# One load queue, some exponentials over four banks, and a new task list in a transformer layer with segment memory

## The chip, the cores and the metric

The kernel runs on one core of a Trainium2 chip. The core has five engines that each work through an instruction queue of their own: TensorE (PE, matrix products), VectorE (DVE), ScalarE (ACT, functions such as exp and tanh), GpSimd (POOL) and SyncE (SP, which here only issues DMA transfers). They are held together by semaphores. Matrix products read SBUF, the on-chip memory, and write PSUM, eight banks of 512 fp32 numbers on each of 128 partitions. ACT can issue DMA transfers too, and while it does so it computes nothing.

The metric is the device time of one execution in microseconds (us). Three runs of the kernel before gave 301.33, 301.71 and 301.79 us; the median is 301.71.

## The reference

One sequence of 2048 tokens, 640 wide, in bf16. A layer with two residual steps:

```python
h  = x + attention(layernorm(x))          # 32 heads of 20, output projection wo
h2 = h + silu(layernorm(h) @ w1) @ w2     # w1: 640 x 1728, w2: 1728 x 640
```

The attention treats the sequence as four segments of 512 tokens, one after the other. In each segment and head

```python
a_dot = softmax(causal(q @ k.T / sqrt(20))) @ v
a_mem = (phi(q) @ M) / (phi(q) @ z + 1e-6)       # phi(t) = t + 1 if t > 0 else exp(t)
o     = sigmoid(beta) * a_mem + (1 - sigmoid(beta)) * a_dot
M    += phi(k).T @ v ;  z += sum(phi(k))
```

so a segment needs the memory `M`, `z` of the segments before it, and nothing else from them.

## The kernel before

**Blocks and segments.** Tokens are held in 16 blocks of 128; segment s holds blocks 4s to 4s+3. The normalised tokens are transposed so that the 640 features lie on partitions (`hT`, `xT`: five chunks of 128). Blocks 0 to 3 are transposed on PE against an identity tile (`n1_tp`, L783) and evicted from PSUM (`n1_te`, L792); all later ones by DMA transposes that SP issues (`n1_tr`, `n2_tr`, L798).

**Heads.** 32 heads of 20 do not fit 32-row strips evenly, so the query and key weights are rearranged on arrival (`re_wq0` to `re_wk4`, `rearr` L678, the copies at L697 and L699): the 20 columns of 20 heads go to five chunks of four strips each, and the columns of the other 12 heads fill the remaining 12 rows of each strip. After a projection (`pr`, L861; segment 0 in two halves of 256 tokens, `x` and `y`) and its eviction (`qe`, L869 on ACT, L870 on DVE), small DMA copies gather these 12 "virtual" heads into their own tile (`vt`, `virt` L900, the transfer at L901; tile `w_sb` in segment 0, `QKV` after it). So there are eight head groups of four heads; groups 0 to 4 read the projections directly, groups 5 to 7 wait for the copies.

**A visit.** For a head group and some key blocks, `scores` (L921) writes the scores of four heads into four PSUM banks side by side (`qk`, L938), ACT takes their exponential into SBUF (`e`, L949), POOL zeroes the part above the diagonal (`mk`, L960). The exponential of a visit is two instructions, one for banks 0 and 1 and one for banks 2 and 3, of 2 x 512 or 2 x 384 numbers. `av` (L981) multiplies with the values, `oe` evicts and scales (L994 on ACT, L996 on DVE), `tn` (L1010, L1014) adds the memory part and turns tokens back onto partitions, `nm` divides (L1027 to L1047), `ad` (L1055, POOL) adds both parts. Segment 0 is visited in halves (`0x` to `7x`, then `0ya`, `0yb` to `7yb`); segments 1 to 3 as `8a, 8b, 8e` and so on, with `8 + g` for group g of segment 1. There are 84 visits.

**Memory.** `pha`, `phb` and `ex` form phi of queries and keys; `kt` transposes phi(k) by DMA, `mz` (L1103) multiplies it with the values, `ma` adds to the fp32 memory, `mb` (POOL, L1139) masks it with constants (`mt`, `mm`, `mzc`) that POOL builds once.

**Back.** `ot` transposes the attention output by DMA (L1156), `wo` projects it (L1164), `rs` adds the residual, `n2_` normalises, `h1` (L1199, its narrow tail L1193) and `th`, `s` (L1208, L1214) form the silu, `h2` (L1241) and `o` (L1254) finish, `out` stores (L1259). `v` (L826) and `ve` (L836, L837) are the value projection and its eviction.

**The order.** Nothing is scheduled by the machine. `ORDER` is one written list of some 1,480 task names; `schedule` (L287) takes them in this order, and each engine gets its tasks in the order in which the list names them. A name may carry an engine (`/A` ACT, `/D` DVE, `/G` POOL, `/S` SP) and, after a colon, the slots (PSUM banks or buffers) that its results take. Names of different engines that stand side by side need not run at the same time. `Tracker.add` puts in the semaphore waits that the data and the slots demand. `fill36` and the like are matmuls of zeros (L618) that keep PE at work.

**The loads before.** SP issues x0, the query weights, the first 384 rows of the key weights, the first 384 rows of the value weights, x4 to x7, `wo`, `beta` and later loads. ACT issues x1, x2 and x3, the other 256 rows of the key weights and the other 256 of the value weights, ahead of its first computation.

Of the kernel before, what the change touches and what calls it, by code (L numbers as in the profile page):

```python
# [1316 lines left out]
```

## Time and profile before

| | |
|---|---|
| median of three runs | 301.71 us |
| span of the profiled execution, first to last instruction | 300.4 us |
| PE busy | 288.8 us, 96% |
| ACT busy | 223.1 us, 74% |
| DVE busy | 222.4 us, 74% |
| POOL busy | 142.7 us, 48% |
| read from and written to HBM | 10.41 MB, 2.62 MB |
| share of the chain that ended last | PE 77%, DVE 12%, DMA 4%, ACT 3% |

The profile is of one execution. Its device time as the runs count it is not given apart; the median of the runs stands 1.3 us above its span, which covers what lies ahead of the first instruction and behind the last. The rows of a stretch give its length and then the busy time of PE, of PE's weight loads, of DVE, ACT and POOL, the granted clock, the busy share of the DMA engines and GB/s. In a list in order of time a row has start, length, engine, line, operation, tiles, shapes and how many instructions were merged; in brackets stands how long the engine was idle before and what ended that. PE's rows overlap, since a matmul's end is modelled with its way through the array; a row of several matmuls, divided by their number, tells what one costs in a stream. "SPq" and "ACTq" are the two queues' DMA issues.

### The profile page before, as it was taken

The page shows a single profiled execution, that of the slowest core. Times are in us where ns is not written, and L with a number is a line of the kernel's source. Part 1 is how long each engine was busy: PE and PEld are TensorE (multiplying, and loading weights), DVE is VectorE, ACT ScalarE, POOL GpSimd, SP SyncE. Part 2 cuts the span into 40 slices and gives each one's busy share as a digit, 9 for nine tenths or more (in the row PEclk, how much of TensorE's full clock was granted, in tenths as well). Part 3 has the DMA queues.
Part 4 walks back from the last instruction along what each step waited for, and adds up shares of the span by engine and source line. Part 5 has one row for each costly group of instructions (what it writes and reads, how often), then busy time and mean ns, then how long its engine had stood idle before and what let it go on. Part 6 is the DMA issues. An engine that isn't in the chain of part 4 may idle for free.

```text
span 300.4 us, 7527 instructions
## 1 busy us (share of the span) xinstructions
PE 288.8 (96%) x2999; PEld 171.4 (57%) x3023; DVE 222.4 (74%) x515; ACT 223.1 (74%) x318; POOL 142.7 (48%) x272
## 2 busy tenths in 40 slices
PE   7799899999999999999999999999999999999996
PEld 5576455455665555556654454566565557764574
DVE  6899988878569689989588866857947787735622
ACT  1898999999998999999589999978777840015400
POOL 6689743534635646855455455564673531200000
PEclk9999999999999999999999999999999999999999
DMA  7994544325454301251742300243120023230002
GB/s 256 362 350 77 116 117 126 89 56 135 85 88 102 63 2 19 42 95 23 94 138 44 79 9 20 39 85 78 47 65 24 2 44 68 46 86 23 0 9 81
DMA packets 49250, 24.66 MB, mean 82 GB/s; under 512 B 39168, under 2 KB 47616, under 8 KB 49216
## 3 DMA queue, kind: packets, MB, share of 16 engines
q1 hardware_dynamic: 46060, 20.52, 31.0%
q10 hardware_dynamic: 3156, 3.67, 4.0%
q8 instruction: 24, 0.39, 0.5%
q14 instruction: 10, 0.08, 0.1%
HBM read 10.41 MB, written 2.62 MB: 43 GB/s over the span
## 4 chain that ended last, share of the span: by engine, by line
PE 77%; DVE 12%; DMA 4%; ACT 3%; issue 2%; SPq 0%; POOL 0%; DVEq 0%; ACTq 0%
PE ps_all L1241 21%; PE ps_all L1199 16%; PE ps_all L861 9%; PE ps_all L1164 8%; PE ps_all L938 7%; PE ps_all L981 6%; PE ps_all L826 5%; DMA sT<-in_A_wk_dram 3%; PE ps_all L1010 2%; ACT PT L949 2%; PE ps_all L1014 2%; PE ps_all L1103 2%; DVE stt L747 2%; DMA oT<-otok 1%; DVE on L1047 1%
## 5 line engine op out<-in xcount | busy, mean ns | idle before, releaser
L949 ACT ACTIVATE PT<-ps_all 128x1024 bf16<-128x1024 f32 (+1 forms) x168 | 157.0, 992 | 15.2 <-PE ps_all L938 13.6
L960 POOL TENSOR_SCALAR_AFFINE_SELECT PT<-PT 128x512 bf16<-128x512 bf16 x128 | 82.7, 649 | 66.9 <-ACT PT L949 63.4
L1241 PE MATMUL ps_all<-w_sb,sT 128*128 128x320 bf16 (+2 forms) x462 | 65.1, 295 | 0.0
L1199 PE MATMUL ps_all<-hT,w_sb 128*128 128x512 bf16 (+1 forms) x314 | 61.6, 335 | 1.5 <-DVE sT L1214 0.4
L1208 ACT ACTIVATE th<-ps_all 128x512 f32<-128x512 f32 (+2 forms) x70 | 34.9, 517 | 36.1 <-PE ps_all L1199 27.4
L1241 PEld LDWEIGHTS ps_all<-w_sb,sT 128*128 128x128 bf16 x462 | 43.3, 98 | 18.9 <-issue 2.1
L1214 DVE SCALAR_TENSOR_TENSOR sT<-th,ps_all 128x512 bf16<-128x512 f32 (+2 forms) x70 | 37.8, 558 | 14.9 <-ACT th L1208 14.2
L1199 PEld LDWEIGHTS ps_all<-hT,w_sb 128*128 128x128 bf16 x325 | 29.6, 98 | 24.9 <-issue 2.8
L1254 DVE SCALAR_TENSOR_TENSOR x_tok<-ps_all,x_tok 128x640 bf16<-128x640 f32 (+3 forms) x18 | 13.3, 748 | 22.4 <-PE ps_all L1241 22.3
L747 DVE BATCH_NORM_STATS2 stt<-x_tok 128x6 f32<-128x320 bf16 x62 | 27.1, 479 | 2.3 <-DMA x_tok<-in_A_x_dram 2.0
L768 POOL TENSOR_TENSOR rst<-rst,eps_c 128x1 f32<-128x1 f32 x32 | 18.3, 573 | 15.4 <-DVE rst L762 13.6
L1164 PE MATMUL ps_all<-wo_sb,oT 128*128 128x320 bf16 x160 | 24.1, 300 | 0.2
L1055 POOL TENSOR_TENSOR otok<-on 128x320 bf16<-128x320 bf16 x24 | 19.0, 799 | 11.0 <-DVE on L1047 11.0
L981 PE MATMUL ps_all<-PT,Vx 128*32 128x256 bf16 (+3 forms) x576 | 23.5, 287 | 0.7 <-DVE Vx L837 0.3
L1047 DVE TENSOR_TENSOR on<-ps_all,rd 128x640 bf16<-128x640 f32 x24 | 19.8, 824 | 0.8
L1164 PEld LDWEIGHTS ps_all<-wo_sb,oT 128*128 128x128 bf16 x160 | 14.8, 98 | 7.8 <-issue 2.0
L870 DVE CAST QK<-ps_all 128x512 bf16<-128x512 f32 x23 | 15.7, 685 | 4.7 <-PE ps_all L861 4.3
L996 DVE TENSOR_SCALAR oTs<-ps_all,lsc 128x512 bf16<-128x512 f32 (+1 forms) x28 | 17.0, 618 | 2.2 <-PE ps_all L981 2.1
L826 PE MATMUL ps_all<-wv_sb,xT 128*128 128x320 bf16 x120 | 18.3, 299 | 0.3 <-ACT Vx L836 0.3
L981 PEld LDWEIGHTS ps_all<-PT,Vx 128*32 128x32 bf16 x576 | 12.2, 96 | 11.1 <-issue 5.1
L774 DVE TENSOR_SCALAR xn_rot<-x_tok,mvt,rst 128x640 bf16<-128x640 bf16 x32 | 15.2, 477 | 4.1 <-POOL rst L768 3.5
L861 PE MATMUL ps_all<-xT,wqr 128*128 128x512 bf16 x69 | 17.2, 379 | 0.7 <-DVE otok L1029 0.2
(88 smaller groups left out, 351.0 us busy)
## 6 DMA issues: line engine op xcount, KB each, us to landing
w_sb<-in_B_w_dram SPq DMA_DIRECT2D x5, 432.0 KB, 9.3
w_sb<-in_B_w_dram SPq DMA_DIRECT2D x3, 480.0 KB, 3.8
out_dram<-x_tok SPq DMA_DIRECT2D x9, 160.0 KB, 1.9
x_tok<-in_A_x_dram SPq DMA_DIRECT2D x2, 640.0 KB, 11.5
out_dram<-x_tok ACTq DMA_DIRECT2D x6, 160.0 KB, 1.8
QKV<-QK SPq DMA_DIRECT2D x12, 72.0 KB
sT<-in_A_wq_dram SPq DMA_DIRECT2D x1, 800.0 KB, 7.6
wo_sb<-in_A_wo_dram SPq DMA_DIRECT2D x1, 800.0 KB, 13.8
```

The lines of the kernel that those rows point to most:

```text
L747: T.add(DV, lambda e, hh=hh: e.bn_stats(out=stt[:, s, 6 * hh:6 * hh + 6], in_=xb[:, 320 * hh:320 * hh + 320]), reads=R((xa, xsub)), writes ...
L826: fns.append(lambda e, c=c, hh=hh: e.matmul(bank(ps, hh)[:, 0:320], lhsT=xT_[:, c, 128 * i:128 * i + 128], rhs=wv_sb[:, c, 320 * hh:320 * ...
L861: fns = [lambda e, kc=kc: e.matmul(bank(ps)[:, lo:hi], lhsT=wt[:, kc, c, :], rhs=xT_[:, kc, lo:hi], start=(kc == 0), stop=(kc == NC - 1)) ...
L949: T.add(AC, lambda e: e.activation(out=pt[:, pta.slot, q0:q0 + 2, 0:width], in_=sc3[:, b0:b0 + 2, 0:width], func=ACT.Exp, scale=SCALE), re ...
L960: T.add(PO, lambda e: e.affine_select(out=v, in_=v, pattern=[[0, 4], [1, 128]], compare_op=ALU.is_ge, fill=0.0, base=0, channel_multiplier ...
L981: fns.append(lambda e, j=j, r=r, h=h, pa=pa, pt=pt, co=co, q0=q0, ji=ji: e.matmul(bank(po)[32 * r:32 * r + 32, q0:hi], lhsT=Vx[:, vx.slot, ...
L1047: T.add(DV, lambda e: e.tensor_tensor(out=on[:, ona.slot, :, :].rearrange("p b (x e) -> p b x e", e=DH), in0=v[:, :, :, 0:DH], in1=r2.unsq ...
L1164: fns.append(lambda e, c=c, hh=hh: e.matmul(bank(ps, hh)[:, 0:320], lhsT=oT[:, c, 128 * i:128 * i + 128], rhs=wo_sb[:, c, 320 * hh:320 * h ...
L1199: fns = [lambda e, c=c: e.matmul(bank(ps)[:, lo:hi], lhsT=w1_sb[:, c, 128 * f:128 * f + 128], rhs=hT[:, c, lo:hi], start=(c == 0), stop=(c ...
L1208: T.add(AC, lambda e: e.activation(out=th[:, tha.slot, lo:hi], in_=bank(ps)[:, lo:hi], func=ACT.Tanh, scale=0.5), reads=R((ps, [0])), writ ...
L1214: T.add(DV, lambda e: e.scalar_tensor_tensor(out=sT[:, f, lo:hi], in0=th[:, tha.slot, lo:hi], scalar=1.0, in1=bank(ps)[:, lo:hi], op0=ALU. ...
L1241: fns.append(lambda e, f=f, t0=t0, fr=fr, hh=hh, n=n: e.matmul(bank(pa, hh)[:, 0:n], lhsT=sT[:, f, t0:t0 + 128], rhs=w2_sb[:, fr, c0 + 320 ...
```

## The change

1. All loads of the head are issued by SP, in the order x0, x1, query weights, key weights (one transfer in place of two), x2 and x3, value weights (still two), then x4 to x7, `wo`, `beta`. ACT issues none of them. In segment 0 the value projection waits for the first part of the value weights ahead of its first six matmuls and for the second part ahead of the other four, instead of for both at once.
2. A name such as `e2x+` in the list stands for one exponential over all four banks of the visit; the pairs `e2x0`, `e2x2` are then gone. 45 of the 84 visits are written so.
3. `ORDER` is another list. PE's tasks keep their order in the main, with the head and the last output blocks arranged differently; `fill12` is gone, `fill2` stands at the end, with a `fill5`. On DVE, ACT, POOL and SP many tasks have other places, 59 tasks have another engine (eight `qe` from ACT to DVE and seven the other way, nine `oe`, seven `vt` from SP to ACT and two the other way, the loads of x12 and of the first part of `w2` from ACT to SP, others), and banks and slots differ.

```diff
 ORDER = """
-halfc:0 epsc iota mt2 x1:3 vpad1 zpad sel w2z/G:0 x0:7 w_q:0 epsg0 mt0 mta0 x2:5,0 w_k1 w_k0 w_wv1:0 warm n1_st3/A:0,0
-n1_st0/D:1 n1_st1/D:6 mtb0 mm0 n1_r0/G n1_r1/D n1_ap0:0 n1_ap1:1 n1_st2/D:2 mm2 n1_r2/D re_wq0/D:0 re_wq2/D n1_r3/G
...
+zpad:0 iota fill36:1 warm x0:7 x1:0 w_q:0 w_k x2:4,1 w_wv0:0 epsc n1_st1/D:3,0 halfc n1_r1/D w_wv1 n1_st0/A:5 n1_r0/D
+sel x4:2,10,3,5 w_wo:0 n1_ap1:1 n1_tp1:2 n1_te1/A:0 beta n1_ap0:0 mt2 n1_tp0:0 n1_te0/A re_wq4/D:0 pr040x:1 qe040x/A:0
+re_wq1/D re_wq0/D pr010x:0 re_wk2/A:0 re_wq3/D re_wq2/D pr000x:4 qe010x/A:0 qe000x/A:0 re_wk1/D pr011x:5 qe011x/A
+re_wk0/D pr001x:6 qe001x/A mt3 re_wk3/D n1_st2/D:1 n1_r2/G mt1 qk1x0:0 e1x2:4 pr021x:7 qe021x/A:0 e1x0 n1_st3/D:5
+n1_ap2:3 mt0 pr030x:6 qk0x0:2 pr020x:7 qe030x/A:0 e0x2:0 n1_r3/D re_wk4/D n1_tp2:0 qe020x/D n1_ap3:2 n1_te2/D pr041x:6
...
+mk10b_384 kt10:0 n1_ap8:0 phb100 ex121:0 h2_1_1 mk11a_0 vt11/S n1_tr8 qk11b0:2 phb120 n1_ap11:3 n1_tr9 n1_tr11 e11b+:6
+mk10e_256 mk11b_0 pha121:2 rs3 n2_st3:7 tn8:0 nm8:0,0 ex141:1 h2_1_2 h2_1_3 o1 mb04:0 mzc2 mb01:0 qk12a0:2 wo2:0
+e12a+:0 ex140:2 av10:6 rs2 oe10/D:0 qk12b0:2 e12b2:5 mz13:7 ma13 phb121 vt14/S vt12/S pr220:0 e12b0 vt16/S qk13a0:4
...
 """.split()
+
+
+ONE_EXP = {row.partition("+")[0] for row in ORDER if row[0] == "e" and "+" in row}
...
     load_x(0, 1, -100, 2.30, "fix", (SP,))
-    load_x(1, 1, -100, 2.33, "fix", (AC,))
-    load_x(2, 2, -97, 4.79, "fix", (AC,))
-    load_w("q", wraw[:, 0, :, :], cw(A_wq), -99, 6.58, [(sT0, ["q"])], "fix", (SP,))
-    load_w("k0", wraw[:, 1, 0:3, :], cw(A_wk[0:384, :]), -99, 4.0, [(sT0, ["k0"])], "fix", (SP,))
-    load_w("k1", wraw[:, 1, 3:5, :], cw(A_wk[384:640, :]), -99, 2.7, [(sT0, ["k1"])], "fix", (AC,))
-    load_w("wv0", wv_sb[:, 0:3, :], cw(A_wv[0:384, :]), -95, 4.96, [(W["wv"], [0])], "fix", (SP,))
-    load_w("wv1", wv_sb[:, 3:5, :], cw(A_wv[384:640, :]), -95, 4.96, [(W["wv"], [1])], "fix", (AC,))
+    load_x(1, 1, -100, 2.33, "fix", (SP,))
+    load_w("q", wraw[:, 0, :, :], cw(A_wq), -96, 6.58, [(sT0, ["q"])], "fix", (SP,))
+    load_w("k", wraw[:, 1, :, :], cw(A_wk), -95, 6.58, [(sT0, ["k"])], "fix", (SP,))
+    load_x(2, 2, -97, 4.79, "fix", (SP,))
+    load_w("wv0", wv_sb[:, 0:3, :], cw(A_wv[0:384, :]), -99, 4.0, [(W["wv"], [0])], "fix", (SP,))
+    load_w("wv1", wv_sb[:, 3:5, :], cw(A_wv[384:640, :]), -99, 2.7, [(W["wv"], [1])], "fix", (SP,))
...
-            rr, ww = [(sT0, ["k0", "k1"] if wi else ["q"])], [(W[k], [c])]
+            rr, ww = [(sT0, ["k"] if wi else ["q"])], [(W[k], [c])]
...
-                T.run(PE, fns, R((xTa, [i]), (W["wv"], [0, 1])), R((ps, [0])))
+                if s == 0:
+                    T.run(PE, fns[:6], R((xTa, [i]), (W["wv"], [0])), R((ps, [0])))
+                    T.run(PE, fns[6:], R((xTa, [i]), (W["wv"], [1])), R((ps, [0])))
+                else:
+                    T.run(PE, fns, R((xTa, [i]), (W["wv"], [0, 1])), R((ps, [0])))
...
-                for q0 in range(r0, r0 + nr, 2):
+                nq = 4 if f"e{name}" in ONE_EXP else 2
+                for q0 in range(r0, r0 + nr, nq):
                     def e_ex(eng, q0=q0, r0=r0, sca=sca):
                         b0 = sca.slot + q0 - r0
-                        T.add(AC, lambda e: e.activation(out=pt[:, pta.slot, q0:q0 + 2, 0:width],
-                                                         in_=sc3[:, b0:b0 + 2, 0:width], func=ACT.Exp, scale=SCALE),
-                              reads=[("ps", b0 + q) for q in range(2)], writes=R((pta, [q0])))
...
+                        T.add(AC, lambda e: e.activation(out=pt[:, pta.slot, q0:q0 + nq, 0:width],
+                                                         in_=sc3[:, b0:b0 + nq, 0:width], func=ACT.Exp, scale=SCALE),
+                              reads=[("ps", b0 + q) for q in range(nq)], writes=R((pta, range(q0, q0 + nq, 2))))
```

The list numbers used below: `n1_st`, `n1_r`, `n1_ap` are a block's statistics (L747, L750 on DVE; L739, L742 on ACT), its reciprocal root (L762 or L765, then the power at L768 on POOL) and the normalisation (L774); `sel` is the identity tile (L633); `w2z` the memset at L601.

198 lines of the change are left out of this document (95 added, 103 removed).

## The prediction

> **What bounds the kernel now.** I read the page's first part, then stretches cut by hand, then the chain of waits, then the first microseconds in order of time.
>
> ```profile
> span 300.4 us, 7527 instructions
> PE 288.8 (96%) x2999; PEld 171.4 (57%) x3023; DVE 222.4 (74%) x515; ACT 223.1 (74%) x318; POOL 142.7 (48%) x272
> ```
> ```profile
> 10.93:29.40 18.47, 17.91 (x184) 13.06 (x184) 18.11 (x61) 17.11 (x35) 16.75 (x52) 1.00 0.93 249
> 29.40:40.00 10.60, 9.05 (x153) 4.84 (x152) 9.86 (x30) 9.94 (x15) 8.41 (x14) 1.00 0.56 126
> 40.00:80.00 40.00, 38.83 (x480) 22.19 (x486) 31.46 (x85) 39.01 (x58) 16.72 (x29) 1.00 0.43 98
> 80.00:130.00 50.00, 48.95 (x568) 28.19 (x571) 40.36 (x88) 47.00 (x65) 29.25 (x46) 1.00 0.31 58
> 130.00:200.00 70.00, 68.91 (x687) 37.49 (x693) 54.35 (x117) 61.81 (x83) 37.56 (x64) 1.00 0.32 58
> 200.00:297.90 97.90, 97.12 (x872) 59.66 (x876) 60.11 (x114) 43.76 (x59) 27.48 (x48) 1.00 0.19 45
> 297.90:300.40 2.50, 0.04 (x1) 0.00 (x0) 0.37 (x2) 0.00 (x0) 0.00 (x0) 1.00 0.35 111
> ```
> The columns are the stretch, its length, then busy time of PE, weight load, VectorE (DVE), ScalarE (ACT) and GpSimd (POOL). PE bounds: it idles 11.6 us in all. From the first projection at 10.93 to the last matmul at 297.9 it idles 0.56 + 1.55 + 1.17 + 1.05 + 1.09 + 0.78 = 6.2 us, 2.97 us lie ahead and 2.46 us behind. But ACT is nearly as full: 9.94 + 39.01 + 47.00 = 95.95 of the 100.6 us from 29.4 to 130, and hardly idle from 29.4 to 80. After 200 it doesn't matter.
>
> ```profile
> 1.71 9.80 DMA sT<-in_A_wk_dram
> 11.53 1.86 DVE wkr L699 x7
> ```
> ```profile
> 1.11 5.51 PE L619 MATMUL ps_all<-zpad 128*128 128x256 bf16 x36 [1.11 <-DVE zpad L596]
> 1.22 1.88 DVE L633 TENSOR_SCALAR ident<-iot 128x128 bf16<-128x128 int32 x1 [0.17 <-POOL iot L631]
> 1.70 1.32 POOL L601 MEMSET w_sb<- 128x1280 bf16 x1
> 2.86 1.28 ACT L598 ACT_TABLE_LOAD   x1 [2.86 <-issue]
> 3.56 0.89 DVE L747 BATCH_NORM_STATS2 stt<-x_tok 128x6 f32<-128x320 bf16 x2 [0.47 <-DMA x_tok<-in_A_x_dram]
> 4.48 0.21 DVE L750 BATCH_NORM_AGGREGATE mvt<-stt 128x2 f32<-128x12 f32 x1
> 7.18 0.73 PE L783 MATMUL ps_all<-ident,xn_rot 128*128 128x128 bf16 x10 [0.56 <-DVE xn_rot L774]
> 7.74 1.47 PE L619 MATMUL ps_all<-zpad 128*128 128x256 bf16 x12
> 7.92 0.74 ACT L739 ACTIVATE otok<-x_tok 128x640 bf16<-128x640 bf16 x1 [3.56 <-DMA x_tok<-in_A_x_dram]
> 9.60 2.08 ACT L792 ACTIVATE hT<-ps_all 128x640 bf16<-128x640 f32 x3
> 9.98 0.45 DVE L774 TENSOR_SCALAR xn_rot<-x_tok,mvt,rst 128x640 bf16<-128x640 bf16 x1
> 10.30 0.55 POOL L768 TENSOR_TENSOR rst<-rst,eps_c 128x1 f32<-128x1 f32 x1
> 10.93 1.26 PE L861 MATMUL ps_all<-hT,wqr 128*128 128x256 bf16 x10
> 13.31 0.50 DVE L699 COPY wqr<-sT 128x400 bf16<-128x400 bf16 x3
> 24.84 1.53 PE L826 MATMUL ps_all<-wv_sb,hT 128*128 128x320 bf16 x10
> ```
> In the first fence (the chain) the head is the key weights' landing at 11.51 and the copies that rearrange them. In the second (order of time), ACT is held by its own five load issues until 2.86, PE runs 36 and then 12 fillers, and useful PE work starts in earnest at 10.93.
>
> **Part 1, one load queue.** Landing times after issue, and what the loads moved (last column, GB/s):
>
> ```profile
> sT<-in_A_wq_dram SPq DMA_DIRECT2D x1, 800.0 KB, 7.6
> sT<-in_A_wk_dram SPq DMA_DIRECT2D x1, 480.0 KB, 9.8
> x_tok<-in_A_x_dram SPq DMA_DIRECT2D x1, 160.0 KB, 2.8
> x_tok<-in_A_x_dram ACTq DMA_DIRECT2D x1, 320.0 KB, 6.7
> ```
> ```profile
> 2.00:5.50 3.50, 3.50 (x25) 2.71 (x24) 2.96 (x7) 1.49 (x2) 2.72 (x8) 1.00 1.01 330
> 12.00:20.00 8.00, 7.57 (x86) 5.72 (x85) 7.90 (x33) 7.55 (x21) 6.70 (x25) 1.00 1.05 351
> ```
> From 12 to 20 us ACT issues no load any more and SP's alone run at 351 GB/s: one queue fills the pipe. In file, query weights end after 160 + 160 + 800 KB = 1.15 MB: at 330 GB/s from 2.0 that is 5.5 us, and x0, first used at 3.56 though its bytes would by that rate be there at 2.5, adds 1.1: 6.6 us. Key weights, 0.82 MB more, about 8.9 in place of 11.5. The other end is the old distance from issue: SP's third issue starts at 1.71 now, its fourth half a microsecond later, so query 1.7 + 7.6 = 9.3 and key 2.2 + 9.8 = 12.0. I take 6.6 and 8.9, since those distances were measured with the other queue's loads between. x1 becomes SP's second load, 1.25 + 2.8 = 4.1; x2 and x3 (7.9 now) come near 10, value weights near 12, wanted by the first value projection at 24.8, so 12 us cover them, and the split wait on them costs nothing.
>
> **Part 2, the head's list.** Statistics of block 1 stay on DVE: 4.1 + 0.9 + 0.2 = 5.2. Those of block 0 go to ACT, free now: 3.56 + 1.7 = 5.3 (block 3's run there from 7.92 until the evictions start at 9.60). Then the identity tile on DVE beside the power on POOL (0.7), the first normalisation 0.45, its transposes 0.36 and some 0.4 of hand-overs: 7.2; then two evictions of 2.08/3 = 0.69, the second block's normalisation and transposes beside the first: hT holds blocks 0 and 1 at 8.6. The chunk-4 copies of query (0.5) fit before. First projection: 8.75, not 10.93; with query at 9.3 it would be 10.1.
> The identity tile (L633) now stands behind r0, in this path. Its only row is 1.88 us, ending 0.08 us after POOL's 1.32 us memset; the nearest DVE row of a small tile, the aggregate, takes 0.21. Bounds 0.2 to 1.88; I take up to 0.7, since beside it POOL has only the 0.55 us powers and no memset. The Trainium skill (SBUF — State Buffer, "SBUF: two separate sides") says that DVE and POOL share a port pair as an exclusive lock and that the loser blocks; the 1.88 us row agrees. By that rule the tile costs about one power, 0.6, an estimate, and the sum stays; by the bare row it costs 1.2 us more than I took, 301.1.
> Between first projection and the visit qk1yb (29.40 now) PE has 18.47 us with 0.56 idle. The new list holds the same twenty half projections, six visits and three value blocks there, and one transpose block more (0.45): 18.36 us of work. Walking it by hand over the DVE copies and ACT evictions, I find waits of some 1.5 us (0.3 before qk1x, 0.3 before the third transpose block, 0.3 before qk4x, the rest between). 8.75 + 18.36 + 1.5 = 28.6: **0.8 us gained**, much less than the 2.2 at the start. The twelve fillers go (1.47 us, in PE's idle time).
>
> **Part 3, one exponential over four banks.** 45 of 84 visits.
>
> ```profile
> 95.21 3.82 ACT L949 ACTIVATE PT<-ps_all 128x1024 bf16<-128x1024 f32 x4 [0.57 <-PE ps_all L938]
> 31.91 1.51 ACT L949 ACTIVATE PT<-ps_all 128x768 bf16<-128x768 f32 x2 [0.16 <-PE ps_all L938]
> ```
> Back to back, 1024 elements take 0.955 us and 768 take 0.755, so 0.78 ns an element and 0.155 us a piece that doesn't scale. A 2048 visit should take 1.75 instead of 1.91 (bounds: 1.51, two of 768, and 1.91, nothing saved). Over 45 visits ACT saves up to 7.0 us. The Trainium skill (ScalarE: Activation LUTs, "What ACT_TABLE_LOAD costs") gives 186 ns + 0.833 ns an element and an overlap of 93 ns; by it 0.09 us goes per visit, 4.2 us in all, an estimate. Against it, five more small copies are issued by ACT (0.7 each, 3.5 us), and two big loads leave it. What stands behind the exponentials gains; a bank that used to come free after the first half waits up to 0.8 us longer, the last one comes 0.16 us sooner. The next visit takes all four banks anyway, so only the one- and two-bank users can lose.
>
> **Part 4, the rest of the list.** PE's order moves little. DVE's does: up to the first second-half visit (qk0ya) the statistics of blocks 7, 9 and 11, 1.1 us each, now come after it, and ACT has five merged visits and no load issues ahead of it, so both reach 29–40 us with some us less to do first. I halve that stretch's idle time: **0.8 us**. Of the 2.2 us idle from 40 to 130 I take **0.4 us**. From 130 on nothing. GpSimd's mask constants move from the head to the end of segment 0's visits, hidden since POOL is 48% busy; without that cover the masks behind them, and the value products behind those, would come late.
> At the end, oT of block 12 is transposed first and block 15 second, while PE still asks for 15 first:
>
> ```profile
> 244.31 5.17 SPq L1156 DMA_TRANSPOSE oT<-otok  x4
> ```
> One issue is 1.3 us; PE has one part of an output block more to do first, so I take a part of it: **0.2 us lost**. The seven last fillers run beside the last store (0.04 of 2.50 us busy now): nothing.
>
> Sum: −0.8 − 0.8 − 0.4 + 0.2 = −1.8: span 298.6. The median of 301.71 stands 1.3 above the profiled span, so **299.9 us**.
>
> **Rivals.**
> *Late copies (slower).* The new list issues the last virtual-head copies of segment 1 (L901) behind three transposes that wait for the output sum o0.
>
> ```profile
> 86.01 0.82 DVE L1254 SCALAR_TENSOR_TENSOR x_tok<-ps_all,x_tok 128x640 bf16<-128x640 f32 x1 [1.19 <-PE ps_all L1241]
> 88.09 0.68 SPq L901 DMA_DIRECT2D QKV<-QK  x1
> 94.07 1.21 SPq L798 DMA_TRANSPOSE hT<-xn_rot  x1
> 96.64 0.40 PE L938 MATMUL ps_all<-QKV 20*128 20x512 bf16 x4
> ```
> 86.0 + 0.8 + 0.5 (normalise) + 3 × 1.2 + 3 × 0.7 = 93.0 for the last issue's end; qk13a reads them at 96.6, 10.6 after o0 starts, in either list. No row has such a copy's landing; at 2.8 from issue (x0) it is there with 1.5 us to spare. At the worst transposed landing of the head,
>
> ```profile
> DMA to landing us min/median/max: 2.7/3.8/7.3
> ```
> 7.3 us, PE waits 3.0 us: 302.9. It decides from 4.3 us. For it: SP's list is full there; against: the DMA engines are 0.31 busy from 80 to 130 (next to last column).
> *ACT is the bound from 29 to 130.* Its 95% busy speaks for it, PE's 97% against. 19 merged visits lie there (e6x to e17b): 19 × 0.155 = 2.9 in place of my 1.2: 298.2.
> *The head buys nothing.* Loads land at the old distance: first projection 10.1, key copies after 12.0, so 0.5 lost instead of 0.8 gained: 301.2.
> *PE cools.* The twelve fillers bridged PE's gap. The first 36 take 0.153 us each, the twelve 0.122: the first start costs 36 × 0.031 = 1.1 us. If the projections had to start so again: 301.0. Against it: the present gap of 1.3 us ahead of the third transpose leaves the first ten projections at 0.126. The Trainium skill (TensorE: Matmul & The Clock Gate, "What's actually happening") puts the fall after an idle window of about 3.4 us; by it the 2.1 us here, with transposes inside, are too short.
> *Four banks held too long.* If four visits cost 0.8 us each on the path: +3.2, 303.1. For it: every merged release is later; against: of the visits' successors on these banks most take all four.
>
> **How the numbers follow.** A measurement of this kernel can't tell less than 0.2%, 0.6 us. Forecast 0.41 (its own range 298.9 to 301.2; 0.39 faster, 0.02 same); ACT bound 0.15, faster; head buys nothing 0.15 (0.05, 0.09, 0.01); late copies 0.19, slower; cooling 0.05 (faster 0.02, same 0.03); banks 0.05, slower. Faster 0.61, same 0.14, slower 0.25. The range runs from below the ACT case to above the bank case, 297.2 to 303.4; for stalls at several places at once it leaves out some 0.1 above.
>
> **What would show it.** Query copies near 7 us and first projection between 8.5 and 9; qk1yb near 28.6; exponentials of 2048 elements near 1.75 us; ACT no longer full from 40 to 80, PE's idle time there under 0.8 us; qk13a waiting for nothing. I am wrong if the first projection waits for weights beyond 10, or if PE's idle time between 29 and 250 grows: then the new list's waits, not its work, decide.

## The result: 302.86 us, 0.5% slower

The changed kernel takes 302.86 us (median of 20 runs, 301.34 to 307.49) against 301.77 for the kernel before on the same chip (20 runs, 301.12 to 302.71): a ratio of 1.0048, 95% interval 1.0025 to 1.0071. I forecast 299.9. Beside the median the scatter is new: the runs before lie within 1.6 us, those after within 6.2.

The first lines of the page of the profiled execution, which took 304.81 us and so is one of the slower half:

```profile
span 303.1 us, 7488 instructions
PE 290.8 (96%) x3016; PEld 171.5 (57%) x3016; DVE 218.8 (72%) x520; ACT 221.2 (73%) x273; POOL 139.4 (46%) x267
```
ACT and DVE have a little less to do than before. The same stretches as in the prediction (stretch, length, busy time of PE, weight load, DVE, ACT, POOL, granted clock, DMA share, GB/s):

```profile
10.93:29.40 18.47, 17.96 (x207) 12.43 (x207) 16.86 (x51) 16.17 (x29) 12.86 (x31) 1.00 0.59 163
29.40:40.00 10.60, 9.58 (x140) 5.41 (x140) 7.93 (x29) 10.26 (x15) 8.39 (x18) 1.00 0.62 151
40.00:80.00 40.00, 38.10 (x475) 21.51 (x468) 32.37 (x84) 36.74 (x46) 18.03 (x37) 1.00 0.57 133
80.00:130.00 50.00, 49.53 (x577) 28.58 (x576) 41.61 (x93) 46.08 (x54) 34.48 (x66) 1.00 0.29 55
130.00:200.00 70.00, 65.87 (x666) 35.12 (x664) 51.62 (x116) 59.92 (x71) 32.11 (x56) 1.00 0.34 60
200.00:297.90 97.90, 97.77 (x877) 59.27 (x875) 61.56 (x124) 46.68 (x55) 31.73 (x52) 1.00 0.23 44
```
PE's idle time is 0.51, 1.02, 1.90, 0.47, 4.13 and 0.13 us, before it was 0.56, 1.55, 1.17, 1.05, 1.09 and 0.78. Two stretches got worse: 40 to 80, and above all 130 to 200, where I had put nothing.

Where the time went is read best from the moments at which PE reaches the same piece of work. Before (a score visit of the head, the output product wo0, a later visit, wo6, wo4, the value block v32):

```profile
29.40 0.34 PE L938 MATMUL ps_all<-w_sb 20*128 20x256 bf16 x8
46.26 1.53 PE L1164 MATMUL ps_all<-wo_sb,oT 128*128 128x320 bf16 x10
51.24 0.34 PE L938 MATMUL ps_all<-w_sb 20*128 20x256 bf16 x8
130.56 1.53 PE L1164 MATMUL ps_all<-wo_sb,oT 128*128 128x320 bf16 x10
134.88 1.53 PE L1164 MATMUL ps_all<-wo_sb,oT 128*128 128x320 bf16 x10
173.20 1.52 PE L826 MATMUL ps_all<-wv_sb,xT 128*128 128x320 bf16 x10
```
After, with the projection pr101 as third row:

```profile
27.57 0.34 PE L942 MATMUL ps_all<-w_sb 20*128 20x256 bf16 x8
44.46 1.53 PE L1169 MATMUL ps_all<-wo_sb,oT 128*128 128x320 bf16 x10
48.42 1.25 PE L865 MATMUL ps_all<-xT,wkr 128*128 128x512 bf16 x5 [1.51 <-DMA xT<-xn_rot]
50.97 0.34 PE L942 MATMUL ps_all<-w_sb 20*128 20x256 bf16 x8
129.03 1.52 PE L1169 MATMUL ps_all<-wo_sb,oT 128*128 128x320 bf16 x10
136.75 1.53 PE L1169 MATMUL ps_all<-wo_sb,oT 128*128 128x320 bf16 x10 [3.35 <-DMA oT<-otok]
175.71 1.53 PE L826 MATMUL ps_all<-wv_sb,xT 128*128 128x320 bf16 x10 [0.78 <-DMA xT<-xn_rot]
```
| reached | before | after | after − before |
|---|---|---|---|
| visit qk1yb | 29.40 | 27.57 | −1.83 |
| wo0 | 46.26 | 44.46 | −1.80 |
| visit qk3yb | 51.24 | 50.97 | −0.27 |
| wo6 | 130.56 | 129.03 | −1.53 |
| wo4 | 134.88 | 136.75 | +1.87 |
| v32 | 173.20 | 175.71 | +2.51 |
| end | 300.4 | 303.1 | +2.7 |

The head alone gains 1.8 us, as much as I had forecast for the whole kernel, and up to 129 us most of it is there. It is lost at three places, and the brackets name the same thing at each: PE waits 1.51, 3.35 and 0.78 us for a transpose by DMA (`xT<-xn_rot`, `oT<-otok`, `xT<-xn_rot`). SP's issues of these transposes before and after (start, time of issue):

```profile
34.73 1.28 SPq L798 DMA_TRANSPOSE xT<-xn_rot  x1
126.94 5.18 SPq L1156 DMA_TRANSPOSE oT<-otok  x4
```
```profile
44.04 1.20 SPq L798 DMA_TRANSPOSE xT<-xn_rot  x1
129.15 2.54 SPq L1161 DMA_TRANSPOSE oT<-otok  x2
171.56 3.44 SPq L798 DMA_TRANSPOSE xT<-xn_rot  x2
```
The three have different histories.
- n1_tr7, the transpose of block 7's normalised rows, is issued at 44.04 instead of 34.73, because the new list puts the block's statistics and normalisation late on DVE:

```profile
41.44 0.88 DVE L747 BATCH_NORM_STATS2 stt<-x_tok 128x6 f32<-128x320 bf16 x2
43.56 0.45 DVE L774 TENSOR_SCALAR xn_rot<-x_tok,mvt,rst 128x640 bf16<-128x640 bf16 x1
```
- ot4 was third of four transposes in a row before, issued at 129.5; now it is the fourth (the second issue of the row at 129.15, so at 130.4), behind ot5 and a copy of a virtual head, although PE asks for block 4 first. How long such a transfer takes from its issue to its landing, least, median and most, before and then after:

```profile
DMA to landing us min/median/max: 2.6/2.7/4.3
```
```profile
DMA to landing us min/median/max: 2.6/2.6/6.3
```
  The 6.3 us are ot4's: 130.4 + 6.3 = 136.7. At the usual 2.6 it had been there at 133.0, and PE was ready at 133.4. So this list leaves ot4 no slack, and any lateness of its transfer is paid in full.
- n1_tr14 is issued at 171.56, because block 14's statistics stand behind block 15's on DVE.

### The profile page after: what moved, and what is told of

Its sections match the earlier page's. It is cut to its first block, busy times and chain, and to the rows that moved or that the text cites. A ratio compares the mean times of both kernels' runs of the same rounds, so it can differ in the third digit from the quotient of the medians.

```text
span 303.1 us, 7488 instructions
## 1 busy us (share of the span) xinstructions
PE 290.8 (96%) x3016; PEld 171.5 (57%) x3016; DVE 218.8 (72%) x520; ACT 221.2 (73%) x273; POOL 139.4 (46%) x267
## 4 chain that ended last, share of the span: by engine, by line
PE 79%; DMA 9%; DVE 7%; ACT 2%; SPq 1%; issue 1%; POOL 0%; DVEq 0%; ACTq 0%
PE ps_all L1246 20%; PE ps_all L1204 18%; PE ps_all L865 13%; PE ps_all L942 7%; PE ps_all L1169 5%; PE ps_all L986 5%; PE ps_all L826 5%; DMA xT<-xn_rot 3%; DMA sT<-in_A_wk_dram 3%; PE ps_all L1015 2%; DMA oT<-otok 2%; ACT PT L954 2%; PE ps_all L1019 2%; PE ps_all L1108 1%; DVE xn_rot L774 1%; DVE Vx L841 1%
## 5 line engine op out<-in xcount | busy, mean ns | idle before, releaser
L954 ACT ACTIVATE PT<-ps_all 128x1024 bf16<-128x1024 f32 (+3 forms) x123 | 153.4, 1284 | 14.0 <-PE ps_all L942 12.9
L965 POOL TENSOR_SCALAR_AFFINE_SELECT PT<-PT 128x512 bf16<-128x512 bf16 x128 | 80.1, 640 | 59.1 <-ACT PT L954 57.2
L1204 PE MATMUL ps_all<-hT,w_sb 128*128 128x512 bf16 (+1 forms) x325 | 62.6, 337 | 0.0
L1213 ACT ACTIVATE th<-ps_all 128x512 f32<-128x512 f32 (+2 forms) x70 | 33.8, 505 | 38.3 <-PE ps_all L1198 20.6
L768 POOL TENSOR_TENSOR rst<-rst,eps_c 128x1 f32<-128x1 f32 x32 | 17.9, 559 | 29.0 <-DVE rst L762 23.8
L747 DVE BATCH_NORM_STATS2 stt<-x_tok 128x6 f32<-128x320 bf16 x62 | 27.2, 480 | 2.8 <-DMA x_tok<-in_A_x_dram 2.5
L874 DVE CAST QK<-ps_all 128x512 bf16<-128x512 f32 x22 | 14.9, 683 | 9.3 <-PE ps_all L865 9.1
L865 PE MATMUL ps_all<-xT,wkr 128*128 128x512 bf16 x75 | 18.7, 380 | 1.5 <-DMA xT<-xn_rot 1.5
L865 PE MATMUL ps_all<-xT,wqr 128*128 128x512 bf16 x75 | 18.5, 380 | 0.0
L1177 DVE TENSOR_TENSOR x_tok<-ps_all,x_tok 128x640 bf16<-128x640 f32 x16 | 13.0, 814 | 7.1 <-PE ps_all L1169 6.9
```

Of the source, the lines that this page charges most:

```text
L747: T.add(DV, lambda e, hh=hh: e.bn_stats(out=stt[:, s, 6 * hh:6 * hh + 6], in_=xb[:, 320 * hh:320 * hh + 320]), reads=R((xa, xsub)), writes ...
L865: fns = [lambda e, kc=kc: e.matmul(bank(ps)[:, lo:hi], lhsT=wt[:, kc, c, :], rhs=xT_[:, kc, lo:hi], start=(kc == 0), stop=(kc == NC - 1)) ...
L954: T.add(AC, lambda e: e.activation(out=pt[:, pta.slot, q0:q0 + nq, 0:width], in_=sc3[:, b0:b0 + nq, 0:width], func=ACT.Exp, scale=SCALE), ...
L965: T.add(PO, lambda e: e.affine_select(out=v, in_=v, pattern=[[0, 4], [1, 128]], compare_op=ALU.is_ge, fill=0.0, base=0, channel_multiplier ...
L1204: fns = [lambda e, c=c: e.matmul(bank(ps)[:, lo:hi], lhsT=w1_sb[:, c, 128 * f:128 * f + 128], rhs=hT[:, c, lo:hi], start=(c == 0), stop=(c ...
L1213: T.add(AC, lambda e: e.activation(out=th[:, tha.slot, lo:hi], in_=bank(ps)[:, lo:hi], func=ACT.Tanh, scale=0.5), reads=R((ps, [0])), writ ...
```

## The experiments

Theory A: the new list's work is not dearer, but it issues three transposes too late for PE; mended, the head's gain comes through. Theory B: these waits are accidents of one execution. Theory C: banks held longer by the merged exponentials cost the time.

| kernel | median us | ratio to before (95%) | profiled span |
|---|---|---|---|
| again | 304.9 | 1.0101 (1.0055 to 1.0147) | 304.5 |
| ot4_first | 301.32 | 0.9986 (0.9964 to 1.0008) | 300.6 |
| tr7_early | 301.7 | 0.9993 (0.9973 to 1.0012) | 303.8 |
| three | 300.0 | 0.9931 (0.9908 to 0.9953) | 298.2 |
| three_split | 300.15 | 0.9953 (0.9935 to 0.9971) | 298.2 |
| three_two_queues | 300.64 | 0.9957 (0.9940 to 0.9974) | 297.7 |
| copies_behind | 301.88 | 1.0009 (0.9991 to 1.0027) | 300.1 |
| before_one_queue | 306.56 | 1.0151 (1.0125 to 1.0177) | 304.7 |
| after_fill | 303.75 | 1.0062 (1.0040 to 1.0084) | 301.4 |
| before_one_exp | 306.09 | 1.0147 (1.0122 to 1.0172) | 303.9 |
| three_copies_behind | 300.24 | 0.9945 (0.9922 to 0.9969) | 298.9 |
| best | 299.96 | 0.9941 (0.9920 to 0.9962) | 298.4 |

The expectations count a landing from the end of its issue, 1.3 us after the issue's beginning. The first four ran on one chip (before: 301.75), the next four on another (301.5), the last four on a third (301.4); across these groups only the ratios compare. Each kernel ran 6 to 13 times.

**again**: the changed kernel, no edit.

> The changed kernel once more, unedited, for a second profile and more times. Theory A (late transposes): the wait of the projection pr101 for block 7's transpose (1.5 us) and of v32 for block 14's (0.8 us) come back, since the list itself issues those transposes late; the wait of wo4 for the transpose ot4 (3.3 us) comes back only where that transfer again takes 5.0 us and not the usual 1.4, so it is between 0 and 3.4 us, and the span follows it: 303.1 with it, 299.7 without. Median 302.9. Theory B (accidents of one execution): the 1.5 and 0.8 us waits are gone or elsewhere. Theory C (four banks held longer is what costs): PE's waits for exponentials are what comes back.

The waits came back at the same places: 1.6 us for n1_tr7, 3.0 for ot4, 1.0 for n1_tr14. So B falls. The median of its six runs is 2 us above what I expected. Part of the reason is in the wo4 row and in the clock behind it (the last three columns are clock, DMA share, GB/s); the three runs at a mean clock of 1.00 still took 303.6 to 303.9, and what they lost no profile shows.

```profile
136.50 2.85 PE L1168 MATMUL ps_all<-wo_sb,oT 128*128 128x320 bf16 x10 [2.95 <-DMA oT<-otok]
```
```profile
136.00:137.00 1.00, 0.50 (x2) 0.29 (x3) 0.00 (x0) 0.00 (x0) 0.93 (x3) 0.58 0.67 129
137.00:138.00 1.00, 1.00 (x5) 0.61 (x4) 0.00 (x0) 0.00 (x0) 0.55 (x1) 0.50 0.08 16
139.00:140.00 1.00, 1.00 (x8) 0.73 (x7) 0.61 (x1) 0.00 (x0) 0.00 (x0) 0.71 0.58 92
```
The ten products of wo4 take 2.85 us instead of 1.53: TensorE's granted clock is 0.50 for about 3 us behind the wait. The wait is paid, and then some 1.5 us more. Of the first 20 runs of the changed kernel the six with a mean granted clock under 1.00 (0.989 to 0.994) took 304.6 to 307.5 us, the other fourteen 301.3 to 304.8. The wait, longer or shorter, and the clock behind it are most of the scatter, as ot4_first and three bear out.

**ot4_first**: two neighbours of the list swapped.

```
-e17a+:2 pha240:0 ot5 ot4 wo4:4
+e17a+:2 pha240:0 ot4 ot5 wo4:4
```


> The changed kernel with two neighbours of its list swapped: ot4 is transposed before ot5, as PE asks for block 4 first. Theory A: ot4 is issued at 129.2 and landed by 132, before PE is ready for it at 133.4; the 3.3 us wait is gone, the slow half of the runs goes with it: median 301.5 (301.2 to 302.0), highest below 303.5. Rival B (the copies around it slow whichever transpose stands there, and the wait only moves): wo5 now waits, median 302.5 to 303. Rival C: nothing changes, 302.9.

```profile
132.38 1.52 PE L1168 MATMUL ps_all<-wo_sb,oT 128*128 128x320 bf16 x10
134.16 1.53 PE L1168 MATMUL ps_all<-wo_sb,oT 128*128 128x320 bf16 x10
```
wo4 follows wo7 without a wait, and the late place in the row is now ot5's (5.3 us to landing), which PE wants 2.9 us later. The median is 301.32, as theory A has it; the rival's new wait at wo5 did not come. One run of twelve, at 303.88 and a clock of 0.994, stands above the 303.5 that I gave as highest. By the ratios (0.9986 against 1.0048) one swap of two words is worth 1.9 us, and 3.6 us against the median of again on the same chip.

**tr7_early**: block 7's statistics, normalisation and transpose earlier.

```
 nm4x:2
+n1_st7:3
 tn1x:7 e6x+:3 w_w1_4:0 ve11/D:1 mk3x_256
+n1_r7/G
...
 ma02/D:0 av5x:7
+n1_ap7:3 n1_tr7
 oe5x/D:0
```
(and the four taken out at their old places between av0y and pr101).

> The changed kernel with block 7's statistics, normalisation and transpose moved ahead of segment 0's first-half visits, nearer to where the kernel before has them (transpose issued near 38 instead of 44). Theory A: pr101 starts at 46.9 and waits for nothing, 1.5 us less to there; the statistics now stand in DVE's 33 to 38 us and may give 0.3 back. If nothing behind gives it back, median 301.5; the wait of wo4 for ot4 is untouched, so the scatter stays, and if that wait is set by DVE's and GpSimd's time rather than by PE's, part of the 1.5 is given back there: 301.3 to 302.9. Rival (DVE is the bound in 30 to 44 us): pr101 gains less than 0.5 us, median 302.5 to 303.

The transpose is issued at 38.03, pr101 starts 1.0 us earlier than in the changed kernel and wo6 0.85 us. The wait for ot4 stays, in this execution at 3.4 us, with the clock halved behind it; median 301.7, highest 305.9. As expected in kind: the gain comes, 1.0 of the 1.5 us in the profile, and the scatter stays.

**three**: both edits, and block 14's statistics ahead of block 15's, its root and normalisation and transpose right behind.

```
-n1_ap13:0 n1_st15:4
+n1_ap13:0 n1_st14:2
...
-v30:5 n1_st14:2
+v30:5 n1_r14/G n1_st15:4
...
-av21:1 s1_6_0 mk20a_0 n1_r14/G n1_r15/G av20:6 n1_ap14:3
+av21:1 n1_ap14:3 n1_tr14 s1_6_0 mk20a_0 n1_r15/G av20:6
...
-e23a+:4 n1_tr14 v32:0
+e23a+:4 v32:0
```


> All three late transposes mended: the two edits above, and block 14's statistics ahead of block 15's with its transpose issued right behind. Theory A: none of the three waits is left, so the profiled 303.1 goes to 303.1 - 1.5 - 3.3 - 0.8 = 297.5, median 299.0 to 300.0, and the runs lie within 1.5 us of each other: the forecast gain of 1.8 us is there once the transposes are in time. Rival (the waits only cover others that stand right behind them: copies of virtual heads, normalisations, ACT): median 301 to 302.

```profile
27.57 0.34 PE L941 MATMUL ps_all<-w_sb 20*128 20x256 bf16 x8
44.91 1.53 PE L1168 MATMUL ps_all<-wo_sb,oT 128*128 128x320 bf16 x10
49.83 0.34 PE L941 MATMUL ps_all<-w_sb 20*128 20x256 bf16 x8
128.04 1.52 PE L1168 MATMUL ps_all<-wo_sb,oT 128*128 128x320 bf16 x10
132.34 1.53 PE L1168 MATMUL ps_all<-wo_sb,oT 128*128 128x320 bf16 x10
170.83 1.52 PE L825 MATMUL ps_all<-wv_sb,xT 128*128 128x320 bf16 x10 [0.21 <-DVE on L1051]
```
Against before: −1.83, −1.35, −1.41, −2.52, −2.54 and −2.37, and −2.2 at the end. The head's gain is kept (0.45 of it is given back at 37.8 us, where PE waits 0.75 us for a mask of POOL and 0.16 in the changed kernel: block 7's root now stands on POOL ahead of the masks), 1.1 us are gained on the way to 128, and nothing is lost after. 300.0 us with all six runs between 299.89 and 300.57. Theory A holds, and this version beats both kernels. The edit for block 14 never ran alone, so its share is not shown.

**three_split**: in that kernel, each of the 45 exponentials over four banks cut in two.

```
-qk12a0:2 wo2:0 e12a+:0
+qk12a0:2 wo2:0 e12a0:0 e12a2
```

> The kernel with the three transposes mended, with each of its 45 exponentials over four banks cut into two over two banks again. ACT gets 45 x 0.08 us = 3.6 us more work, by the difference of the busy times of the exponentials before and after (157.0 and 153.4 us). Theory A (the merge helps where ACT is full, from 30 to 130 us, in which 19 of them lie): 0.3 to 1.5 us slower than 300.0, so 300.3 to 301.5. Theory C (banks held longer cost on the path): faster than 299.7. If both are small: 299.8 to 300.3.

The total of the exponentials, after and split:

```profile
L954 ACT ACTIVATE PT<-ps_all 128x1024 bf16<-128x1024 f32 (+3 forms) x123 | 153.4, 1284 | 14.0 <-PE ps_all L942 12.9
```
```profile
L955 ACT ACTIVATE PT<-ps_all 128x1024 bf16<-128x1024 f32 (+1 forms) x168 | 156.3, 987 | 13.2 <-PE ps_all L943 12.5
```
2.9 us of ACT's time, and PE's end is the same: both profiled spans are 298.2. The two ran on different chips; by the ratios (0.9953 against 0.9931) the split is 0.7 us slower, with intervals that overlap. So in this list the merge brings little, and whether it is nothing or some tenths of a microsecond these runs can't tell. It doesn't cost anything: C falls for the changed kernel.

**before_one_exp**: the kernel before with the same 45 visits merged, in the place of the second half.

```
-qk12a0:2 e12a2:5 e12a0 mk12a_0
+qk12a0:2 e12a+:5 mk12a_0
```


> The kernel before with the same 45 visits' exponentials done once over four banks, in the place of the second half; the rest as it was. ACT saves 45 x 0.08 = 3.6 us. Theory A, after the split of the mended kernel cost 0.15: no difference that can be told, 301.2 to 301.8. Rival (ACT is the bound from 29 to 130): 300 to 301. Theory C (banks held longer, and the list was made for halves): 302 to 303.5.

4.7 us slower. The rows of the waits in one stretch:

```profile
61.42 0.72 PE L1200 MATMUL ps_all<-hT,w_sb 128*128 128x256 bf16 x5 [1.01 <-ACT PT L950]
64.47 0.34 PE L938 MATMUL ps_all<-w_sb 20*128 20x256 bf16 x8 [0.48 <-ACT PT L950]
```
PE waits for exponentials (L950) where it waited for none before: at 61.42 a matmul of the first feed-forward layer, which takes one bank, waits 1.01 us until one exponential has read all four; in the kernel before the same product follows the one ahead of it without a wait. PE's longer waits for exponentials add up to 3.6 us here, and the profiled span is 3.5 us longer. In only three of the 45 visits does other ACT work stand between the halves, so it isn't the place in ACT's order. C is true for the list that was made for halves. It is false for the one searched with the merge.

**before_one_queue**: the kernel before with the loads on one queue, the load lines as in the change, and its list only so far changed:

```
-x0:7 w_q:0 epsg0 mt0 mta0 x2:5,0 w_k1 w_k0 w_wv1:0 warm
+x0:7 x1:3 w_q:0 w_k x2:5,0 w_wv0:0 w_wv1 epsg0 mt0 mta0 warm
```
(x1 and w_wv0 are taken out at their old places).

> The kernel before with the loads of the head alone changed: one queue in the order x0, x1, query, key weights whole, x2 and x3, value weights; the rest of its list as it was. Theory A: the weights land earlier (query near 8.2, key near 10.5), but in this list the first projection waits for the statistics and normalisations in DVE's order (first projection 10.93), so little is gained: 301.2 to 301.8. Rival (the loads alone bring the head's 1.8 us): 299.9 to 300.9. Rival (blocks 2 and 3, landed at 11 instead of 8, hold the third transposes): 302 to 303.

The largest miss of all runs. DVE's and PE's rows of the head:

```profile
10.84 0.89 DVE L745 BATCH_NORM_STATS2 stt<-x_tok 128x6 f32<-128x320 bf16 x2 [4.10 <-DMA x_tok<-in_A_x_dram]
13.41 0.71 PE L781 MATMUL ps_all<-ident,xn_rot 128*128 128x128 bf16 x5 [4.57 <-DVE xn_rot L772]
```
Blocks 2 and 3 land at 10.8 instead of 7.9. In this list the transposes of block 2 stand on PE ahead of the first projection, and DVE waits 4.1 us for that load before block 2's statistics: PE waits 4.6 us for the normalised rows, loses 4.2 by the first value block, and carries them to the end (4.3 at the last output products of segment 2). (ACT waits for the same load, with block 3's statistics ahead of the evictions of hT.) The third branch of the expectation, at four times its price, with the clock lowered as well (0.988 to 0.994 as a mean in all six runs; 0.50 from 13 to 18 us in the profile, behind the wait). The delay in the head passes to the end one for one here.

**three_two_queues**: the mended kernel (three) with the load lines of before, on SP's and ACT's queues.

```
-x0:7 x1:0 w_q:0 w_k x2:4,1
+x0:7 x1:0 w_q:0 w_k0 w_k1 x2:4,1
```

> The same mended kernel with the loads of the head on two queues as before the change (x1, x2 and x3, the second parts of key and value weights on ACT's queue, key weights in two pieces). Theory A (one queue brings the weights in the order of their use): query weights land near 8.8 instead of 8.2 and key weights near 11.5 instead of 10.5, so PE is 0.6 to 1.5 us later at the first visit and stays so: median 300.6 to 301.5. Rival (the head's gain is the new list's, statistics on ACT and an earlier first normalisation, and the queue matters little): 299.9 to 300.3.

```profile
8.48 1.81 PE L865 MATMUL ps_all<-hT,wqr 128*128 128x256 bf16 x15 [1.11 <-ACT hT L792]
```
A miss: query weights landed at 6.6 and key weights at 9.4, earlier than on one queue (8.2 and 10.5 in the profile after, 7.5 and 9.8 in that of three), and the first projection began at 8.48. The head's gain comes with the list: it is there on two queues too. The median is not lower; the runs scatter again (298.95 to 301.33). In the profiled execution, which took 299.41 us, ot5 landed 4.5 us after its issue's end and wo5 waited 0.3 for it; what the slower runs lost no profile shows.

**copies_behind**: the changed kernel with vt22, vt27 and vt28 behind ot4, ot5 still first.

```
-e18b+:5 vt22/S qk17a0:0 pha210:0 rs7 vt28/A mk18b_0 pha220:0 e17a+:2 pha240:0 ot5 ot4 wo4:4
+e18b+:5 qk17a0:0 pha210:0 rs7 mk18b_0 pha220:0 e17a+:2 pha240:0 ot5 ot4 vt22/S vt28/A vt27/S wo4:4
```

> The changed kernel with the three copies of virtual heads that stand between and beside the transposes of oT (vt22, vt27, and vt28 on ACT's queue) moved behind ot4; ot5 stays ahead of ot4. ot4 is then issued 0.7 us earlier, at 129.7. Theory D (what makes ot4 land 5.0 us after its issue is the small packets of these copies on the same DMA engines): it lands 1.4 to 2.5 us after its issue, by 133.4, the wait of wo4 is gone or under 0.5 us, median 301.3 to 301.9. Theory E (the last of four transposes in a row lands late whatever else is moved; the fourth took 3.0 in the kernel before and 4.1 and 2.6 in the two mended kernels): it lands 3 to 5 us after, the wait stays at 1 to 3 us, median 302 to 303.

```profile
133.83 1.53 PE L1168 MATMUL ps_all<-wo_sb,oT 128*128 128x320 bf16 x10 [0.56 <-DMA oT<-otok]
```
```profile
DMA to landing us min/median/max: 2.6/2.7/4.3
```
Between the two theories: 4.3 us to landing instead of 6.3, a wait of 0.56 instead of 3.35, median 301.88, one run above 302.7. With the copies among the transposes, ot4 as the fourth landed 5.9 to 6.4 us after its issue's beginning in four profiles (after, again, tr7_early, after_fill), so some 2 us of its lateness go with the copies; it is late even so, like the slowest in the kernel before (4.3). But in the mended kernel the slowest of the four took 3.9 (three) and 2.7 us (three_split) with the copies in place, and 4.5 with the copies behind (three_copies_behind): the copies alone don't decide it, and what else does stays open.

**after_fill**: 24 multiplications by zeros ahead of wo4 in the changed kernel.

```
-pha240:0 ot5 ot4 wo4:4
+pha240:0 ot5 ot4 fill24:4 wo4:4
```


> The changed kernel with 24 multiplications by zeros (2.6 us) ahead of wo4, where TensorE waits 3.0 to 3.4 us for the transpose ot4. Theory F (TensorE's granted clock is halved by the idle stretch itself: in two of three profiles it is 0.50 for some 3 us behind the wait, and wo4's ten products take 2.6 to 2.9 us instead of 1.5): with at most 0.8 us idle the clock stays at 1.00 in every run and the halving's 1.5 us go, so no run above 304; where ot4 is early the fillers cost up to 2.6 us. Median 302.5 to 303.3. Rival (the clock falls for another reason, as power): some runs still show 0.994 or less and 305.

All nine runs are at a granted clock of 1.00, where six of the first 20 and three of the six of again were under it: as theory F has it, it is the idle stretch that lets the clock fall. Two runs stand above 304 (304.18 and 304.31), where I had expected none, and the median of 303.75 is 0.45 above my range; probably the fillers cost time also where ot4 lands early, but the profiled execution is one in which it landed late. And wo4 is not the only place: a mean clock of 0.994 also occurs once each in ot4_first and three_copies_behind and twice in the 23 runs of the kernel before on this chip, in executions that have no profile.

**three_copies_behind** and **best**: the mended kernel with the copies behind ot5, on one queue and, in best, with three_two_queues' loads.

```
-e18b+:5 vt22/S qk17a0:0 pha210:0 rs7 vt28/A mk18b_0 pha220:0 e17a+:2 pha240:0 ot4 ot5 wo4:4
+e18b+:5 qk17a0:0 pha210:0 rs7 mk18b_0 pha220:0 e17a+:2 pha240:0 ot4 ot5 vt22/S vt28/A vt27/S wo4:4
```

> The mended kernel, with vt22, vt27 and vt28 moved behind ot5 too, so that the four transposes of oT stand together. PE has the third of them in time already; the last, ot5, lands by 133 and is wanted at 135.2. Theory A: nothing left to gain there, 299.8 to 300.2.

> The three transposes mended, the four transposes of oT together ahead of the copies, and the head's loads on two queues as before the change. In the mended kernel with two queues the query weights landed at 6.6, v00 began at 22.5 instead of 23.4 and the span was 297.7 although wo5 waited 0.4 us for ot5; without that wait 297.3, median 299.0 to 299.8, and closer together than 298.95 to 301.33. Rival (two queues scatter in the head itself): 300.3 to 300.8 with the same scatter.

300.24 and 299.96 on one chip, ratios 0.9945 and 0.9941: no difference by the queue, none to three either. best scatters less than three_two_queues (299.33 to 300.54), but the half microsecond more that I expected of it isn't there: its first projection began at 9.62 in the profiled execution, 8.48 in that of three_two_queues, with the loads on the same two queues. What differs there is the time of PE's 36 products of zeros, as the next section shows.

## Why the prediction was wrong, step by step

**The sum.** It had −0.8 for the head, −0.8 for 29 to 40, −0.4 for 40 to 130, nothing behind, +0.2 at the end. Measured by the table: −1.8, 0.0, then +1.5 and −1.3, then +3.4 and +0.6 and +0.2. From 29.4 to 297.9 us PE's idle time grew from 5.6 to 7.7 us, which the prediction had named as a sign that it is wrong.

**The step that failed** is part 4: "From 130 on nothing", where 4.2 us were lost, and the 0.8 + 0.4 us that 29 to 130 was to gain, where 0.3 were lost, with a wait of 1.5 for block 7's transpose in it. I compared how much work stands ahead of a place on each engine, and read "the statistics of blocks 7, 9 and 11 … now come after it" as time given to DVE. It was that, and it also took the slack from what the statistics lead to: normalisation, transpose by SP, landing, projection. Block 7's transpose cost 1.5 at 48 us. (The 0.8 us of the stretch ahead of it are another matter: −1.83 at its start, −1.80 at 46, and in three, where the transpose is early, −1.35. PE's idle time there is 1.64 us, before 1.61, in waits of at most 0.5 us for values, masks and virtual heads. Less to do on DVE and ACT did not shorten it.) For ot4 I had walked only the four transposes at the end (block 12 before block 15), where the order turned out to cost nothing: PE idles 0.13 us from 200 on, so the 0.2 were not lost. The same exchange one segment earlier, ot5 ahead of ot4, I did not look at, and it was worth 1.9 us by the ratios of ot4_first.

**The idle time I wanted to win back** was partly not there. The page before has 2999 matmul records to 3023 weight loads, the page after 3016 to 3016: 24 products have no record, and their time counts as idle. Yet 40 to 130 gave more than the 0.4 I took, once pr101 is out of the way: 1.3 us from qk3yb to wo6, 1.1 in three.

**Part 1, one queue.** Query weights at 8.2 and key weights at 10.5, not 6.6 and 8.9; the other ends were 9.3 and 12.0. One queue moved less at the start; before and after:

```profile
0.00:8.00 8.00, 6.33 (x49) 4.90 (x50) 5.13 (x12) 1.57 (x3) 5.09 (x20) 1.00 0.78 263
```
```profile
0.00:8.00 8.00, 6.69 (x46) 5.11 (x46) 2.52 (x9) 3.66 (x7) 1.81 (x11) 1.00 0.73 220
```
263 GB/s on two queues, 220 on one (260 and 262 in the other two profiles on two queues, 221 to 242 in the others on one). The 330 that I used was itself a rate of two queues, and the 351 that of a later stretch. In this profile it cost little: the first projection waited for hT, and the copies of the key weights then held PE for 0.23 us. But in two of the nine profiles of the new list on one queue (ot4_first and three_copies_behind) the query weights came at 8.9 and 8.6 and held the first projection, by some 0.8 us:

```profile
9.56 1.80 PE L864 MATMUL ps_all<-hT,wqr 128*128 128x256 bf16 x15 [1.93 <-DVE wqr L698]
```

**Part 2, the head's list.** First projection 8.93 (forecast 8.75), but by another way, so that the nearness is partly luck. Both normalisations were done at 6.57. The transposes still stood behind the 36 products of zeros, which the sum had left out:

```profile
1.12 6.13 PE L619 MATMUL ps_all<-zpad 128*128 128x256 bf16 x36 [1.12 <-DVE zpad L596]
7.09 0.72 PE L783 MATMUL ps_all<-ident,xn_rot 128*128 128x128 bf16 x10
```
In the profiles of the new list these 36 take 5.7 to 6.8 us, and where the weights are there in time the first projection begins 1.8 us behind the transposes, between 8.48 and 9.62. Why their time varies, no run here shows. The identity tile took 0.22 us:

```profile
4.92 0.22 DVE L633 TENSOR_SCALAR ident<-iot 128x128 bf16<-128x128 int32 x1
```
That is the lower end of my bounds, and the 0.7 that I took was too much. The sentence from the Trainium skill (SBUF — State Buffer, "SBUF: two separate sides") is not tested by this row: no memset ran beside it now, and POOL's first power began at 5.01, behind the tile's start. In the kernel before, too, the tile began ahead of the memset to which I had put its 1.88 us (1.22 and 1.70), so what made it long is not shown. What I mis-sized are the waits between first projection and qk1yb: 1.5 forecast, 0.26 measured (18.64 us, of which PE is busy 18.38):

```profile
8.93:27.57 18.64, 18.38 (x188) 13.17 (x189) 16.74 (x57) 15.56 (x27) 11.09 (x28) 1.00 0.64 190
```
So the term is −1.8 and not −0.8.

**Part 3, the exponentials.** By form, after and before (count, busy time, mean ns):

```profile
L954 ACT ACTIVATE PT<-ps_all 128x2048 bf16<-128x2048 f32 x38 | 71.4, 1879 | 8.4 <-PE ps_all L942 7.9
```
```profile
L949 ACT ACTIVATE PT<-ps_all 128x1024 bf16<-128x1024 f32 x136 | 132.7, 1033 | 13.1 <-PE ps_all L938 12.2
```
1.88 us for 2048 elements against 2 × 132.7/136 = 1.95: 0.07 saved, not 0.16. In all 157.0 − 153.4 = 3.6 us, half of my 7.0 and near the 4.2 that follow from the Trainium skill (ScalarE: Activation LUTs, "What ACT_TABLE_LOAD costs"): by its fixed part and rate 2048 elements take 1.89 us, and the trace has 1.88; my slope between 768 and 1024 elements was wrong. That only bank users between the visits could lose was right, and before_one_exp shows the price, 4.7 us, where the list isn't made for it.

**The rivals.** Late copies: qk13a waited for nothing, so that its 302.9 us lie at the measured 302.86 is chance; but the mechanism (SP's order lets something land too late for PE) was the right one, at other transfers. Banks held too long: not in this list. ACT as the bound from 29 to 130: the split of the 45 exponentials gave ACT 2.9 us more and left the profiled span where it was, so not as a bound; some tenths of a microsecond stay possible. The head buys nothing: it bought 1.8. Cooling: not in the head, where I had put it, but behind the ot4 wait.

## What to carry to other kernels

When a list of work is reordered, follow each transfer that feeds the bounding engine, not the sums ahead of a place: note its landing and its consumer's start before and after, and mistrust every one whose slack falls under the spread of its landing time, here 2.6 to 6.4 us. A merge of operations or a move of loads belongs with the list that was made for it: the merge cost 4.7 and the single queue 5.1 us in the old list, and in the new one neither costs anything that the medians can tell. And idle time read from a trace should first be held against missing records.

## What the hardware showed that I had not expected

The granted clock of TensorE fell to 0.50 for about 3 us behind idle stretches of 2.95 us (again) and 3.40 us (tr7_early) and stayed at 1.00 behind one of 3.35 us (the first profile). The Trainium skill (TensorE: Matmul & The Clock Gate, "What's actually happening") has a free-running window of 3.4 us; that the same wait is punished in one execution and not in the next agrees with free-running, but 2.95 us are less than a window, and the runs decide: three idle microseconds can be enough.

A transpose by DMA of the same 128 × 640 tile landed between 2.6 and 6.4 us after its issue began. In the row of four at 130 us with copies of virtual heads among them, the slowest took 5.3 to 6.4 us in six profiles and 3.9 and 2.7 in two; with the copies behind, 4.3, 4.5 and 2.8. And the query weights landed at 6.6 and 6.9 us on two queues and between 7.2 and 8.9 on one, in lists with the same head.
